# A planned long-convolution kernel with a second plan: order of the calls, large slots, PSUM rooms and the engine of its flexible copies

## The chip, the cores and the metric

The kernel runs on one core of one Trainium2 chip. The metric is the time in device microseconds (us) of one execution; the median of three runs is taken. A core has engines that work beside one another, each with its own queue of instructions: TensorE (PE, matrix products; "PEld" is the loading of its weights), VectorE (DVE), ScalarE (ACT), GpSimd (POOL) and SyncE (SP, which here only issues DMAs). SBUF is the on-chip memory of 128 partitions, PSUM the smaller memory into which PE writes and from which DVE or ACT must copy.

## The reference

The input u has 2048 positions and 448 channels. Two long convolutions of it are mixed by a gate:

```
g = sigmoid(sum(u * gate_w))                                  # per position
K = real(sum_n C_n * exp(dt * A_n * l) * dt * B_n)            # S4 kernel, 256 modes, l = 0..2047
a = causal_conv(u, K) + u * Dskip                             # "A"
kv = shift_conv(k, shift_k) * v                               # 4 taps
b = u * (causal_conv(kv, ssm_k) + kv * ssm_D)                 # "B"
out = g * a + (1 - g) * b
```

The causal convolutions are 2048 long; the reference does them by an FFT of twice that length.

## The kernel before, in words

**Work.** The 448 channels lie in four partition groups of 112; each convolution is done in four passes H = 0 to 3 of NC = 28 channels per group. `PLAN` (L37) gives the stages: T0 to T3 make the S4 kernel K of a pass, B0 to B3 are the passes of convolution B, A0 to A3 those of A, and four mixes m join the two.

- A **table** (`table`, L921; `KGen` L433, `Part` L520): 16 exponentials on ACT; four levels, each of phases on DVE, a Sin on ACT and a magnitude on DVE; products on DVE that fill the tables TQ and TP; then `sums` (L632), 448 small matmuls from TP and TQ, in seven groups of 64; then `gather`, matmuls that put the sums in order, and their copies. T3 is made in two halves. Exponentials and Sin need different tables on ACT, so each crossing has an ACT_TABLE_LOAD.
- A **convolution** (`conv_B` L911, `conv_A` L944): `spread` and `transform` (matmuls, each group ended by a copy from PSUM), `swapped` (copies of halves of the partitions over SP's DMA queue), `products` on DVE (two of 3584 elements), `stage_a` with copies, `stage_b` with an epilogue on DVE that uses the gate or u and writes back into natu or natv. A3, at the end, writes out in pieces (`store`, L890), half on SP's and half on ACT's queue.
- The **head**: modes and constants are loaded and prepared (`Consts` L176, `Modes` L650); DVE's first work needs c_pidx (L181), an iota of GpSimd. k is loaded by four transposing DMAs on SP (L774), three into natu and one into a large slot, with v and the kernel of B behind them on the same queue. The short convolution (L839) is eight groups of 56 matmuls, each ended by a DVE product with v into natv; natu is then free and u is loaded there.
- The **gate** (L858 to L871): one DVE product of 3584 elements (gwt), 112 matmuls, a copy (gx), one matmul, a Tanh on ACT and a scaling on DVE (gt). The first pass of A needs gt.

**What sets the order.** The program doesn't issue its calls as it makes them. `Order` (L125) notes all 6479 calls of all engines in a list, and `issue` (L132) issues them in the sequence of the string `ORDER`, whose numbers are places in that list; L137 is where each is issued, and so it is the line of nearly all instructions in the profile. Calls of one engine run in that sequence; between engines only semaphores for true dependences hold. `SLOTS` says for each of 54 large tiles which of seven SBUF slots q0 to q6 (3584 bf16 elements per partition) it takes (`Places.slot`, L153), and `ROOMS` says for each of 209 groups of matmuls which of four PSUM rooms of two banks it uses (`Places.room`, L157). `SIDES` says for each of 208 copies or scalings whether DVE ("V") or ACT ("S") does it (`Sides`, L336): copies of a room to SBUF, the phase's second half (`ahead`) and the sign of a level (`minus`).

The seven slots and four rooms tie the engines: a group of matmuls can start only when its room has been emptied, and a slot is written only when its last reader is done.

Of the kernel before, what the change touches and what calls it, by code (L numbers as in the profile page):

```python
# [35 lines left out]
NSLOT = 7  # L36
PLAN = (("T", 0), ("B", 0), ("B", 1), ("T", 1), ("B", 2), ("A", 0), ("T", 2), ("B", 3), ("A", 1), ("T", 3), ("A", 2), ("m", 0), ("m", 1), ("m", 2), ("m", 3), ("A", 3))  # L37
SLOTS = (
    "201031456232433120056615532041060303231061540604265013"
)  # L40
ROOMS = (
    "031230120122130132023010223312031201320001012121201100302332131110331210203301002313130323111031203103303210320132212000"
    "13111112310221033031032020012311212323010303033031323212102022201023121232131202010303130"
)
SIDES = (
    "SVSSSSSVSSSSSSSSSSSSSSSSSSSSSSSVSSSVSSVSSSSSSSSSSSSSSSSSSVVVVVSSSSSSSSSSSSSSSSSSSSSSSSSSSSSSSSSSSSSSSSSSSSSVVVVSSSSSSSSS"
    "SSSSSSSSSSSSSSSSSSSSSSVSSSSSSSSSSSSSSVSVVSVVSSSSSSVSSSSSSSSSSSVSSVVSSSSSSSSSVSVSVSSSVSSS"
)
ORDER = (
# [54 lines left out]
)  # L104

def after(tc, ins, before):
# [906 lines left out]
```

## Time and profile before

| what | value |
|---|---|
| median of the runs | 261.9 us (261.25, 261.9, 261.94) |
| span of the profiled execution | 257.9 us |
| instructions | 12431 |
| first DVE instruction, end of the last | 3.06 us, 247.6 us |
| end of the last matmul | 246.3 us |
| DMA | 26.44 MB, mean 103 GB/s |

The profile is of one execution; its span leaves out about 4 us that the runs' time includes. "Busy" is the time in which an engine has an instruction at work; since PE's matmuls are pipelined, its busy time isn't its peak. A row of a group gives the engine, the operation, out<-in by the program's names, the shapes, the count, then the busy time and the mean of one in ns, and the idle time of the engine ahead of it with what ended that. A row of a timeline begins with the start and the length in us. A row of the windows view gives the stretch, its length, and for each engine the busy time and the number of instructions, then the granted clock of PE (1.00 is full), the DMA share and GB/s.

### The profile page before, as it was taken

The page shows a single profiled execution, that of the slowest core. Times are in us where ns is not written, and L with a number is a line of the kernel's source. Part 1 is how long each engine was busy: PE and PEld are TensorE (multiplying, and loading weights), DVE is VectorE, ACT ScalarE, POOL GpSimd, SP SyncE. Part 2 cuts the span into 40 slices and gives each one's busy share as a digit, 9 for nine tenths or more (in the row PEclk, how much of TensorE's full clock was granted, in tenths as well). Part 3 has the DMA queues.
Part 4 walks back from the last instruction along what each step waited for, and adds up shares of the span by engine and source line. Part 5 has one row for each costly group of instructions (what it writes and reads, how often), then busy time and mean ns, then how long its engine had stood idle before and what let it go on. Part 6 is the DMA issues. An engine that isn't in the chain of part 4 may idle for free.

```text
span 257.9 us, 12431 instructions
## 1 busy us (share of the span) xinstructions
PE 208.9 (81%) x5631; PEld 188.6 (73%) x5631; DVE 237.4 (92%) x378; ACT 199.5 (77%) x278; POOL 30.5 (12%) x81
## 2 busy tenths in 40 slices
PE   0634784988779999998889998989999998999820
PEld 0511484978669898997879887888899897998810
DVE  4999999999999999999999999988999999998830
ACT  2299993089979999999999999989999975653300
POOL 8970001200000002100000021000031120000000
PEclk9995596899979999999999999997999999999975
DMA  6999983499861347475043055600462375120088
GB/s 167 212 164 216 165 178 74 82 171 159 139 157 32 47 106 144 79 167 91 7 99 104 3 102 95 149 24 3 111 110 38 57 145 131 29 51 4 3 163 125
DMA packets 58917, 26.44 MB, mean 103 GB/s; under 512 B 49520, under 2 KB 57200, under 8 KB 58864
## 3 DMA queue, kind: packets, MB, share of 16 engines
q1 hardware_dynamic: 52192, 18.65, 39.5%
q0 software_dynamic: 2160, 5.51, 12.2%
q10 hardware_dynamic: 4512, 1.49, 3.0%
q8 instruction: 44, 0.72, 1.2%
q14 instruction: 9, 0.07, 0.1%
HBM read 8.17 MB, written 2.52 MB: 41 GB/s over the span
## 4 chain that ended last, share of the span: by engine, by line
DVE 61%; PE 17%; issue 6%; DMA 5%; ACT 5%; SPq 1%; POOL 1%; DVEq 0%; ACTq 0%; POOLq 0%
DVE TP L137 18%; PE ps L137 17%; DVE q L137 15%; DVE TQ L137 15%; DVE natv L137 5%; ACT q L137 3%; DMA TP<-TP 3%; DVE ET L137 3%; DVE G L137 2%; DVE RK L137 1%; SPq L137 1%; DMA q<-q 1%; ACT ET L137 1%; DMA sk<-in_B_ssm_k_dram 1%; DVE hold L137 1%
## 5 line engine op out<-in xcount | busy, mean ns | idle before, releaser
L137 ACT CAST q<-ps 128x1024 bf16<-128x1024 f32 (+4 forms) x151 | 126.6, 929 | 23.9 <-PE ps L137 23.1
L137 PEld LDWEIGHTS <-q 128*128 128x128 bf16 (+2 forms) x720 | 52.3, 147 | 13.5 <-DMA q<-in_A_A_re_dram 8.4
L137 DVE TENSOR_TENSOR TQ<-TQ,ET 128x896 bf16<-128x896 bf16 (+2 forms) x70 | 45.5, 687 | 0.1
L137 PEld LDWEIGHTS <-natu 128*32 128x32 bf16 (+1 forms) x560 | 30.6, 183 | 8.9 <-issue 7.2
L137 PE MATMUL ps<-TP,TQ 128*32 128x32 bf16 x1792 | 33.3, 240 | 4.1 <-DVE TQ L137 2.6
L137 PE MATMUL ps<-q,s_W 128*128 128x112 bf16 (+1 forms) x544 | 33.8, 214 | 3.5 <-ACT q L137 3.4
L137 PE MATMUL ps<-sa_R,q 128*128 128x128 bf16 x448 | 33.3, 229 | 2.4 <-DVE q L137 1.0
L137 PEld LDWEIGHTS <-TQ 128*32 128x32 bf16 x1792 | 30.1, 153 | 6.7 <-DVE TQ L137 3.1
L137 DVE TENSOR_TENSOR q<-q,q 128x3584 bf16<-128x3584 bf16 (+1 forms) x22 | 32.4, 1513 | 1.2 <-ACT q L137 1.2
L137 PEld LDWEIGHTS <-s_W 128*128 128x128 bf16 x544 | 28.2, 100 | 6.5 <-issue 4.5
L137 DVE TENSOR_TENSOR TP<-TP,ET 128x1792 bf16<-128x1792 bf16 (+3 forms) x25 | 31.4, 1275 | 0.1
L137 POOL DMA_DIRECT2D TP<-TP x15 | 13.1, 914 | 153.8 <-PE ps L137 89.6
L137 PEld LDWEIGHTS <-G 128*128 128x128 bf16 x1024 | 27.9, 96 | 4.3 <-issue 2.5
L137 PE MATMUL ps<-q,G 128*128 128x28 bf16 x1024 | 28.5, 175 | 1.4 <-ACT q L137 1.4
L137 ACT ACTIVATE q<-hold 128x224 bf16<-128x224 f32 x64 | 22.4, 414 | 5.0 <-DVE hold L137 5.0
L137 PE MATMUL ps<-q,natu 128*32 128x336 bf16 (+3 forms) x336 | 17.8, 334 | 5.7 <-DVE natv L137 4.2
L137 ACT ACTIVATE ET<-q 128x1344 bf16<-128x1344 int16 (+1 forms) x12 | 17.2, 1457 | 1.4 <-DVE q L137 1.3
L137 PE MATMUL ps<-q,q 128*32 128x336 bf16 (+3 forms) x112 | 17.8, 334 | 0.0
L137 PE MATMUL ps<-Wc,natu 128*64 128x128 bf16 x224 | 15.5, 285 | 0.6 <-DVE q L137 0.6
L137 ACT CAST RK<-ps 128x448 bf16<-128x448 f32 (+1 forms) x16 | 11.5, 742 | 5.4 <-PE ps L137 5.4
L137 DVE TENSOR_TENSOR TQ<-TQ 128x448 bf16<-128x448 bf16 (+2 forms) x35 | 15.3, 446 | 0.1
L137 DVE CAST q<-ps 128x1024 bf16<-128x1024 f32 (+3 forms) x13 | 12.6, 978 | 2.4 <-PE ps L137 1.4
(81 smaller groups left out, 276.6 us busy)
## 6 DMA issues: line engine op xcount, KB each, us to landing
q<-q SPq DMA_DIRECT2D x64, 112.0 KB, 3.1
TP<-TP POOLq DMA_DIRECT2D x9, 448.0 KB, 5.0
natv<-in_B_v_dram SPq DMA_DIRECT2D x4, 448.0 KB, 7.3
sk<-in_B_ssm_k_dram SPq DMA_DIRECT2D x16, 112.0 KB, 3.8
natu<-in_A_u_dram SPq DMA_DIRECT2D x4, 448.0 KB, 10.2
TP<-TP POOLq DMA_DIRECT2D x6, 224.0 KB, 3.8
out_dram<-natv SPq DMA_DIRECT2D x8, 112.0 KB, 4.6
out_dram<-natv ACTq DMA_DIRECT2D x8, 112.0 KB, 4.5
```

The lines of the kernel that those rows point to most:

```text
L137: ins = f(*args, **kw)
```

## The change

Four strings are replaced, and nothing else: `SLOTS`, `ROOMS`, `SIDES` and `ORDER`. The calls and the PLAN stay; the same 6479 calls are issued in another order. In `SIDES` the number of V falls from 28 to 16: 21 copies or scalings go from DVE to ACT, 9 from ACT to DVE. Some of what moves in `ORDER`:

- c_pidx (call 1) stands ahead of the long iota (call 104) on GpSimd.
- T1's exponentials (2238 to 2253) stand among the head's calls on ACT, ahead of the first copies of the convolutions. One group of the short convolution (398 to 453) stands behind the first groups of B0's spread.
- T0's seven groups of sums (880 to 1327) stand in one block; T1's stand in two blocks.
- The gate's product and matmuls (688, 689 to 800) with what follows them (801 to 804) stand among A0's and T2's calls instead of T0's; 3614 is the first gated product of A0.

```diff
--- before.py
+++ after.py
@@ -36,71 +36,68 @@
 NSLOT = 7
 PLAN = (("T", 0), ("B", 0), ("B", 1), ("T", 1), ("B", 2), ("A", 0), ("T", 2), ("B", 3), ("A", 1), ("T", 3), ("A", 2), ("m", 0), ("m", 1), ("m", 2), ("m", 3), ("A", 3))
 SLOTS = (
-    "201031456232433120056615532041060303231061540604265013"
+    "021542305636511452202433460065313202216640354003105642"
 )
 ROOMS = (
-    "031230120122130132023010223312031201320001012121201100302332131110331210203301002313130323111031203103303210320132212000"
-    "13111112310221033031032020012311212323010303033031323212102022201023121232131202010303130"
+    "11223103012210302330220032331212210013320021033131021301111231323102110223230233221201311003220113302301102003222013"
+    "111030323310002132213200232132113303202300232012233311303200120101020221120311012032012033101"
 )
 SIDES = (
-    "SVSSSSSVSSSSSSSSSSSSSSSSSSSSSSSVSSSVSSVSSSSSSSSSSSSSSSSSSVVVVVSSSSSSSSSSSSSSSSSSSSSSSSSSSSSSSSSSSSSSSSSSSSSVVVVSSSSSSSSS"
-    "SSSSSSSSSSSSSSSSSSSSSSVSSSSSSSSSSSSSSVSVVSVVSSSSSSVSSSSSSSSSSSVSSVVSSSSSSSSSVSVSVSSSVSSS"
+    "SSSSSSSSSSSSSSSSSSSSSSSSSSSSSSSSSSSSSSSSSSSSSSSSSSSSSSSSSSSSSSSSSSSSSSSSSSSSSSSSSSSSSSSSSSSSSSSSSSSSSSSSSSSVSVVVSSSS"
+    "SSSSSSSSSSSSSSSSSSSVSSSSSSSSSSSSSSSSSSSSSSSVSVVVSSSSSSSVSSSSSSSSSSSSSSSVSSSSSSSSSSVSSSVVSVVS"
 )
 ORDER = (
-    "35 38 81 0 32-34 1 37 2 67-68 5 106 36 108 31 69 63 225 64 75 210 44 109 76 211 207 15 208 104 41 77 20 105 78 112 83 "
-    "107 74 6 71 202 70 66 212 72 209 73 221 214 50 82 30 65 111 219 110 79 17 140-155 215 84 216 116-117 203 222 91 204 "
-    "220 223 43 160-175 11 157 40 80 156 159 811 810 158 177-192 176 822 821 18 829 61 88 824 831 224 19 46 836 816 830 86 "
-    "809 113 823 805 837 12 194 817 89 808 812 22 120-121 807 14 813 226 806 39 45 85 818 123-124 193 825 4 3 25 130-131 "
...
-    "1536-1543 1844 861 2001-2008 874 62 1544 1967-1982 862 1843 2009 1841 1604-1611 2248 845 1983 1518-1525 865 878 1612 "
-    "1509-1516 866 2000 1622-1629 1526 873 1527-1534 876 1517 1631-1638 1630 688 1546 2010-2017 2238 1548 1613-1620 1639 "
-    "1551 1535 868 2019-2026 1552 867 2246 1842 689-800 2027 1547 2018 1550 870 2239 1545 871 3615 872 879 1549 2259 877 "
-    "2037-2044 875 1621 2270 1136-1199 2269 2271 2260 2045 2264 1264-1327 2262 1845 2272 115 2263 2273 1640-1647 801 2265 "
...
+    "1 104 69 207-208 2 70 214 32 75 63 106 209 216 67 7 108 39 68 64 31 140-147 215 26 210 105 24 211 0 212 19 65 28 "
+    "107 38 221 35 202 213 3 77 222 76 109 71-72 223-224 203 217-218 116 78 112 118 15 66 219 117 119 220 111 33-34 110 "
+    "113 204 22 79 156 805 817 808 37 811 6 807 157 813 819 73 148-155 158 74 159 36 160-175 816 829 20 806 50 837 21 10 "
+    "831 8 836 810 821 16 812 4-5 824 176 830 44 185-192 47 838 225 832 43 809 823 45 177-184 2254 194 29 822 839 193 12 "
...
+    "625 568 818 42 340 842 201 626-682 2249 40 227-282 57 1500-1507 2247 849 3615 2244 283 114 1508 1449-1464 1466-1481 "
+    "1465 1483-1498 1482 851 2262 398-453 511 683 1499 1527-1535 853 454 1844 857 1842 855 2263 1536-1543 1518-1525 "
+    "1587-1602 1526 856 1841 1544 873 1603 1570-1585 58 1586 1509-1517 858 874 1553-1569 2259 1604-1611 861 1612 1547 "
...
+    "2761 3627 3419 2762 688 3472-3479 3025-3040 3438-3453 3629 3421-3436 3645 3041 3454 3654 3652 3657 3659 3646 3480 "
+    "3455-3470 689-800 3661 3437 3658 3471 3663 801 3060-3067 4995 3078-3085 3068 4263 3660 802-803 2990 4264 4282-4297 "
+    "5002 3669 3665 2781-2820 4298 3672 3086 4299-4314 4996 3668 3548-3613 4315 3653 2821 2763-2779 804 2780 3662 3673 "
+    "3614 3051-3059 3664 4265-4280 2984 3069-3076 4281 3481-3546 4998 3077 4997 4999 4316-4324 5000 2839-2854 2822-2838 "
...
+    "5941-6007 6323-6356 6077 6357 6360 6358 6401-6434 6359 6440-6472 6362-6394 6435 6438 6361 6439 6437 6473-6476 6478 "
+    "6395-6396 6400 6436 6398 6397 6399 6477 "
 )
```

84 rows, old and new, of the table ORDER are left out of this document.

## The prediction

> **What bounds the kernel now.** I read the page's busy line and its chain of waits first, then stretches of the span.
>
> ```profile
> PE 208.9 (81%) x5631; PEld 188.6 (73%) x5631; DVE 237.4 (92%) x378; ACT 199.5 (77%) x278; POOL 30.5 (12%) x81
> ...
> DVE  4999999999999999999999999988999999998830
> ACT  2299993089979999999999999989999975653300
> ...
> DVE 61%; PE 17%; issue 6%; DMA 5%; ACT 5%; SPq 1%; POOL 1%; DVEq 0%; ACTq 0%; POOLq 0%
> ```
>
> VectorE (DVE) is the busiest engine and 61% of the chain. But the shares are means over unlike stages, so I cut the span where each table's small matmuls begin on TensorE (PE), by the rows of the tile TQ: T1 at 122.0, T2 at 166.4, the second half of T3 at 219.7 us.
>
> ```profile
> L137 PE MATMUL ps<-TP,TQ x127: 228/242/259, 122.0 to 124.0; 128*32 128x32 bf16 x127
> ...
> L137 PE MATMUL ps<-TP,TQ x44: 227/237/255, 166.4 to 167.0; 128*32 128x32 bf16 x44
> ...
> L137 PE MATMUL ps<-TP,TQ x96: 227/240/263, 219.7 to 221.9; 128*32 128x32 bf16 x96
> ```
>
> The windows view then gives, for each stretch, its length and the busy time of PE, PEld, DVE, ACT and POOL:
>
> ```profile
> 52.48:122.04 69.56, 62.54 (x1619) 57.90 (x1618) 68.41 (x92) 67.30 (x96) 2.59 (x3) 0.98 0.67 117
> 122.04:166.36 44.32, 40.04 (x1173) 36.85 (x1173) 44.14 (x60) 44.26 (x64) 2.56 (x3) 1.00 0.35 76
> 166.36:219.72 53.36, 50.88 (x1523) 47.57 (x1523) 50.95 (x101) 45.29 (x56) 5.82 (x8) 0.97 0.38 79
> 219.72:246.28 26.56, 25.25 (x776) 23.09 (x773) 23.73 (x29) 11.95 (x17) 0.00 (x0) 1.00 0.12 27
> 246.28:257.90 11.62, 0.00 (x1) 0.00 (x0) 1.33 (x4) 0.00 (x0) 0.00 (x0) 0.59 0.87 146
> ```
>
> No single engine bounds it. From T1 to T2, DVE and ScalarE (ACT) are both full (44.14 and 44.26 of 44.32) and PE loses 4.3 us. From T2 to T3, PE has 50.88 of 53.36: it loses 2.5 us, and ACT has room. In the last stretch PE sets the pace and loses 1.3 us. After PE come 11.6 us of last products and stores. So from T1 on the time is PE's work (40.04 + 50.88 + 25.25 = 116.2 us) plus 8.1 us that PE loses. Before T1, PE has 208.9 - 116.2 = 92.7 us of work in 122 us, and DVE, nearly never idle, decides.
>
> **The copies (SIDES).** 21 copies and scalings go from DVE to ACT, 9 go the other way. The groups by form give the prices.
>
> ```profile
> L137 ACT CAST q<-ps 128x1024 bf16<-128x1024 f32 x64 | 64.0, 1044 | 16.6 <-PE ps L137 16.2 <-DVE TP L137 0.3
> L137 ACT CAST q<-ps 128x896 bf16<-128x896 f32 x58 | 51.9, 951 | 4.3 <-PE ps L137 4.2
> L137 ACT CAST q<-ps 128x512 bf16<-128x512 f32 x20 | 12.4, 622 | 0.6 <-PE ps L137 0.4
> L137 ACT ACT_TABLE_LOAD x9 | 11.5, 1283 | 3.3 <-PEq L997 1.7 <-DVE q L137 1.4
> L137 DVE CAST q<-ps 128x1024 bf16<-128x1024 f32 x6 | 7.3, 1222 | 2.1 <-PE ps L137 1.1 <-ACT ET L137 1.0
> L137 DVE CAST q<-ps 128x896 bf16<-128x896 f32 x2 | 2.2, 1080 | 0.0
> L137 DVE TENSOR_SCALAR q<-q 128x672 int32<-128x672 int32 x6 | 3.5, 592 | 0.1
> L137 ACT CAST q<-ps 128x448 bf16<-128x448 f32 x5 | 2.6, 541 | 1.9 <-PE ps L137 1.9
> L137 ACT ACTIVATE ET<-ET 128x672 bf16<-128x672 bf16 x3 | 2.4, 788 | 0.0
> L137 DVE TENSOR_SCALAR ET<-ET 128x672 bf16<-128x672 bf16 x5 | 1.9, 379 | 0.0
> L137 ACT ACTIVATE q<-q,quarter 128x672 int32<-128x672 int32 x2 | 1.8, 875 | 0.0
> L137 DVE CAST q<-ps 128x448 bf16<-128x448 f32 x3 | 1.8, 616 | 0.0
> L137 DVE CAST q<-ps 128x512 bf16<-128x512 f32 x2 | 1.4, 691 | 0.3 <-PE ps L137 0.3
> ```
>
> DVE loses 6 x 1.222 (1024 wide) + 2 x 1.080 + 2 x 0.691 + 2 x 0.616 + 4 x 0.592 + 4 x 0.379 + the small gate copy 0.1 = 16.1 us. It gains one copy of 1024 and one of 896, one of 512, three of 448, one of 768 (between the rows of 512 and 896: 0.69 to 1.08, I take 0.95) and two scalings of 672: 1.22 + 1.08 + 0.69 + 1.85 + 0.95 + 0.76 = 6.6 us. Net -9.5; neighbours overlap by about a twentieth, so I take **-9.0 us for DVE**. ACT gains 6 x 1.044 + 2 x 0.951 + 2 x 0.622 + 2 x 0.541 + 4 x 0.875 + 4 x 0.788 + 0.2 = 17.3, loses 6.6 at its own prices (1.04 + 0.8 + 0.62 + 0.95 + 3 x 0.54 + 2 x 0.79) and, as its new order crosses between two tables once more, gains a tenth table load, 1.3: 12, or with overlap about **+11 us for ACT**. PE's work stays 208.9. DVE's saving lies on a path in the first half; ACT's addition is covered only where ACT has idle time, that is at the head and after 200 us, and not from 122 to 166.
>
> **The head.** The order puts the small iota that DVE waits for ahead of the long one on GpSimd, and T1's 16 exponentials into a stretch where ACT waited.
>
> ```profile
> 0.84 1.99 POOL L137 IOTA TP<- 32x2048 bf16 x1 [0.40 <-POOLq L997]
> 2.90 0.13 POOL L137 IOTA c_pidx<- 128x1 int32 x1
> ...
> 3.06 0.15 DVE L137 TENSOR_SCALAR TP<-c_pidx 128x1 int32<-128x1 int32 x1 [3.06 <-POOL c_pidx L137]
> ...
> 40.89 2.08 DVE L137 TENSOR_TENSOR natv<-ps,natv 128x896 bf16<-128x896 f32 x2
> ...
> 42.03 0.61 PE L137 MATMUL ps<-q,natu 128*32 128x448 bf16 x3 [4.17 <-DVE natv L137]
> ...
> 52.48 2.88 ACT L137 CAST q<-ps 128x1024 bf16<-128x1024 f32 x3 [11.67 <-PE ps L137]
> ```
>
> DVE can start about 2 us earlier. Ahead of its first eviction of the k-shift convolution the new order has 35.3 us of DVE work where the old had 37.3 (summed over the trace's durations). So PE's 4.17 us of idling shrinks, and the eviction itself comes about 3 to 4 us earlier. ACT then starts the convolutions' copies at 45 to 48 instead of 52.5. Against it: the fourth transposed load of k now uses a slot that frees later, and it holds SP's queue (v and the ssm kernel behind it) some 3 to 5 us; with DVE's first eviction at 37 to 39 this stays covered, and it costs up to 3 us if not. Between the ends -7 and -1 at the head I take -4.5.
>
> The clock is the other part of this: the windows after the idle time show half of it.
>
> ```profile
> 42.00:44.00 2.00, 1.97 (x36) 1.67 (x39) 2.00 (x3) 0.00 (x0) 0.00 (x0) 0.50 0.86 163
> ...
> 48.00:50.00 2.00, 2.00 (x80) 2.00 (x75) 2.00 (x2) 0.00 (x0) 0.00 (x0) 1.00 0.93 172
> ```
>
> PE did 36 of these matmuls in 2 us at a granted clock of 0.50, and 80 at 1.00, so the slow stretch cost some 2 us. [...]
>
> **The stages, by PE's work left.** I ran the three sums of busy time through the new order. DVE's work ahead of the end of T1's table falls from 117.2 to 110.8 us: three copies (3.0), the gate's large product, which goes later (2.0), and smaller moves. With DVE 2 us earlier that is 8.4 us; the ring of rooms emptied by ACT, now busy from 46 on, leaves about 4.5. So T1's small matmuls begin at 117.5. But this is partly borrowed: PE has 121.0 us left there instead of 116.2, since the gate's matmuls and a part of the convolutions now stand behind T1.
>
> ```profile
> 65.99 2.01 DVE L137 TENSOR_TENSOR q<-gw,one 128x3584 bf16<-128x3584 bf16 x1
> ...
> L137 PE MATMUL ps<-natu,q 128*32 128x64 bf16 x112 | 3.6, 301 | 0.3 <-ACT q L137 0.3
> ```
>
> If PE lost the same 8.1 us, its end would be 117.5 + 121.0 + 8.1 = 246.6 us, where it is 246.3 now: **no gain at all**. The forecast so hangs on what PE loses.
> - T1 to T2: 48.9 us of PE work, 48.3 of DVE, 48.8 of ACT. Three engines with the same load, and the gate's round (DVE, PE, ACT, PE, ACT, DVE) among them: PE must lose something. Nothing lost is one end, 7 the other (below); I take 3.5, a little under the 4.3 now, since now DVE and ACT have 10% more work than PE there. T2 at 117.5 + 52.4 = 169.9.
> - T2 to T3: PE 48.0, DVE 45.1 (now 50.88 and 50.95). DVE no longer stands level with PE: a loss of 0.5 instead of 2.5. T3 at 218.4.
> - The rest: 24.1 and the same 1.3: PE ends at 243.8.
> - Stores and last products as now, 11.6: span 255.4, or 2.5 us less than 257.9. What ACT gets more behind T2 is covered by its idle time, for it is busy 14.71 and 9.47 us of 20 there:
>
> ```profile
> 200.00:220.00 20.00, 18.86 (x601) 17.30 (x599) 19.63 (x38) 14.71 (x19) 2.58 (x3) 1.00 0.52 108
> 220.00:240.00 20.00, 19.52 (x619) 17.99 (x612) 18.05 (x22) 9.47 (x15) 0.00 (x0) 1.00 0.12 28
> ```
>
> Slots and rooms add no work; their new numbers act by waits alone, and those are in the losses above. The swaps on SP's queue stand behind waits for PE and DVE that the sums put ahead of their readers; if one is late it costs its landing time, 3.1 us by the page's DMA rows:
>
> ```profile
> q<-q SPq DMA_DIRECT2D x64, 112.0 KB, 3.1
> ```
>
> **The rivals.**
> 1. DVE's gain arrives in full: nothing but PE's own work counts from T1 to T3. PE ends at 117.5 + 121.0 + 1.3 = 239.8, span 251.4, run 255.4. For it: DVE has 9 us less to do and is 61% of the chain. Against: DVE alone would allow 257.9 - 9 = 248.9, but PE's 121 us behind T1 do not; and ACT has no idle time from T1 to T2.
> 2. The early gain is given back: PE loses as much as now, 246.6, span 258.2, run 262.2. No change. For it: the sum of DVE's and ACT's work grows by 2 us, and PE's is the same.
> 3. **Slower: ACT is the new pacemaker between T1 and T2.** It has 48.8 us of work there and is also held by the gate: by the sums of busy time ACT reaches the copy of the gate's sums 2.4 us before PE ends its 112 matmuls, and DVE reaches the first gated product of conv A about 4 us before the gate's value is there, and what ACT copies next waits for DVE. If these 6.4 us come on top of ACT's 48.8, T2 begins at 172.7; with losses as now behind it (2.5 and 1.3) PE ends at 172.7 + 50.5 + 25.4 = 248.6, span 260.2, run 264.2. It decides from a T2 later than 170.4 (losses as now behind) to 172.4 (losses of my forecast). For it: ACT stood at 44.26 of 44.32 already; against: the gate's round can be covered by the copies behind it.
>
> **How the numbers follow.** The profiled execution had 257.9 us of span, and the median of the runs is 261.9, so 4.0 us lie around the span; I add the same: 255.4 + 4.0 = 259.4. Two kernels of this length can be told apart from about 0.3%, 0.8 us: faster is under 261.1, slower over 262.7. Chances: my forecast 0.43 (from 257.4 to 261.1), rival 1 0.17, rival 2 0.13, rival 3 0.27. That makes 0.60 faster, 0.13 the same, 0.27 slower. The range goes from rival 1 (255.4, its own spread a little lower) to rival 3: 255.0 to 264.4; left out are about 0.05 below and 0.12 above, where a late swap or the late load of v adds to rival 3. By itself the forecast's range is 257.4 to 261.1.
>
> **What would show it.** In the profile of the changed kernel: DVE about 228 and ACT about 210 busy; DVE's first instruction near 1; the first copy of the convolutions on ACT before 48 and no clock of 0.5 after 38; T1's small matmuls near 117.5, T2's near 170, T3's second half near 218.4, PE's last at 243.8. Wrong would be: a T2 after 172 with ACT's idle time in the 120s put down to PE or DVE (rival 3); a T1 not before 120 (the head's gain lost, as by a late load of v or by ACT); PE idle by over 2 us between T2 and T3 with DVE named.

## The result: the changed kernel is slower, by 22 us

| | before | after |
|---|---|---|
| median of the runs | 261.6 us | 283.8 us (282.8 to 285.7) |
| ratio, 95% interval | | 1.086 (1.080 to 1.092) |
| span of the profiled execution | 257.9 us | 282.6 us |
| first copy of the convolutions on ACT | 52.5 us | 44.3 us |
| small matmuls of T0, T1, T2, second half of T3 begin | 74.0, 122.0, 166.4, 219.7 | 72.0, 127.1, 181.2, 240.6 |
| PE ends | 246.3 us | 272.3 us |

Some executions run slower as a whole, whatever the kernel; the medians and ratios below leave those out.

The forecast was 259.4 us in a range from 255.0 to 264.4. The page of the kernel after, busy times, slices and chain:

```profile
PE 218.3 (77%) x5631; PEld 195.9 (69%) x5631; DVE 229.8 (81%) x366; ACT 212.3 (75%) x291; POOL 30.4 (11%) x81
...
DVE  8999999999929739999867998985839797747950
ACT  5669998999908998999769999935889976356100
...
PEclk9999999959955997999899999997599999869955
...
PE 42%; ACT 29%; DVE 12%; issue 9%; SPq 2%; DMA 2%; ACTq 0%; DVEq 0%; POOL 0%; POOLq 0%
```

DVE has 7.6 us less to do and ACT 12.8 us more, where the sums gave 9 and 11. But DVE's and ACT's rows of digits now have holes, the deepest of them at the same place (2 and 0 tenths in the twelfth slice, 78 to 85 us), and the chain has gone from DVE (61%) to PE (42%) and ACT (29%). The windows view, cut where the tables' small matmuls begin:

```profile
72.00:127.10 55.10, 42.65 (x1177) 39.81 (x1177) 42.97 (x60) 44.55 (x62) 2.56 (x3) 0.85 0.49 93
127.10:181.20 54.10, 48.76 (x1360) 45.23 (x1360) 48.24 (x64) 49.43 (x69) 2.56 (x3) 0.97 0.28 58
181.20:240.60 59.40, 51.09 (x1490) 46.66 (x1489) 45.41 (x90) 44.24 (x56) 5.79 (x8) 0.91 0.35 72
240.60:272.30 31.70, 26.26 (x751) 24.09 (x749) 22.44 (x29) 11.74 (x15) 0.00 (x0) 0.85 0.12 26
```

From T0 to T1 all three engines have 10 us and more of idle time in 55.1 us. Before, that stretch was 48.0 us long and none of the three had more than 2.3 us idle in it:

```profile
74.00:122.04 48.04, 45.81 (x1291) 42.74 (x1291) 46.89 (x64) 45.91 (x69) 2.59 (x3) 0.96 0.50 101
```

So the place to look at is where each of these stretches begins: at the 448 small matmuls of a table. The same windows for the sums of T0, T1 and T2 alone, before:

```profile
74.00:87.70 13.70, 13.17 (x540) 12.01 (x541) 12.58 (x23) 12.19 (x23) 0.00 (x0) 0.88 0.38 79
122.00:132.60 10.60, 9.58 (x473) 8.77 (x474) 10.42 (x21) 10.55 (x11) 0.00 (x0) 1.00 0.13 28
166.40:181.20 14.80, 13.71 (x529) 12.97 (x529) 12.93 (x25) 12.94 (x17) 0.00 (x0) 0.88 0.12 28
```

and after:

```profile
72.00:85.30 13.30, 7.80 (x450) 7.32 (x451) 7.44 (x13) 5.19 (x7) 0.00 (x0) 0.74 0.53 74
127.10:137.10 10.00, 8.42 (x458) 7.88 (x457) 9.37 (x10) 8.42 (x9) 0.00 (x0) 0.83 0.03 7
181.20:194.10 12.90, 9.06 (x466) 8.46 (x466) 8.08 (x13) 5.05 (x5) 0.00 (x0) 1.00 0.10 24
```

The sums take about as long in both kernels. Before, PE did 540 matmuls in T0's 13.7 us, 92 of them other groups, and ACT and DVE worked 12 us beside it. After, PE does the block of 448 and nothing else, 7.8 us of work in 13.3, and ACT works 5.2 and DVE 7.4. The timelines of PE, ACT and DVE at T0's block:

```profile
72.01 2.24 PE L134 MATMUL ps<-TP,TQ 128*32 128x32 bf16 x131 [0.26 <-ACT q L134]
76.91 2.19 PE L134 MATMUL ps<-TP,TQ 128*32 128x32 bf16 x128 [2.66 <-issue]
80.64 2.17 PE L134 MATMUL ps<-TP,TQ 128*32 128x32 bf16 x128 [1.54 <-issue]
84.09 1.12 PE L134 MATMUL ps<-TP,TQ 128*32 128x32 bf16 x61 [1.29 <-issue]
...
85.27 0.54 ACT L134 CAST RK<-ps 128x448 bf16<-128x448 f32 x1 [8.07 <-PE ps L134]
...
85.34 0.63 DVE L134 TENSOR_TENSOR TQ<-hold,ET 128x896 bf16<-128x896 bf16 x1 [5.90 <-PE ps L134]
```

PE does 131 of the small matmuls in 2.24 us, then stands idle for 2.66 with nothing to wait for that the profile shows ("issue"), does 128, stands again, and so on. ACT has emptied its last room at 76.3, has ended all other work by 77.2 and then waits 8.07 us for the sums; DVE has one product left, which ends at 79.4, then waits 5.90 us, for it may not write the next table into TQ before the sums have read it.

(The long iota behind which c_pidx stood is call 81; the section on the change gave 104, which is a DVE call that reads c_pidx. And where that text speaks of seven groups of 64 small matmuls, several groups stand side by side in the kernel before: its runs on PE are 128, 64, 64, 128, 64 long in T0, 192, 64, 64, 128 in T1 and 128, 64, 64, 64, 128 in T2. After, they are 448 in T0, twice 224 in T1 and in T2, and 224 in each half of T3.)

### The profile page after: what moved, and what is told of

It is laid out like the page before. It is cut to its first block, busy times and chain, and to the rows that moved or that the text cites. A ratio compares the mean times of both kernels' runs of the same rounds, so it can differ in the third digit from the quotient of the medians.

```text
span 282.6 us, 12420 instructions
## 1 busy us (share of the span) xinstructions
PE 218.3 (77%) x5631; PEld 195.9 (69%) x5631; DVE 229.8 (81%) x366; ACT 212.3 (75%) x291; POOL 30.4 (11%) x81
## 4 chain that ended last, share of the span: by engine, by line
PE 42%; ACT 29%; DVE 12%; issue 9%; SPq 2%; DMA 2%; ACTq 0%; DVEq 0%; POOL 0%; POOLq 0%
PE ps L134 42%; ACT q L134 21%; DVE TP L134 4%; DVE q L134 3%; ACT ET L134 3%; SPq L134 2%; DVE TQ L134 2%; DMA q<-q 2%; ACT L134 1%; DVE natv L134 1%; ACT s_W L134 1%; ACT TQ L134 1%; DVE natu L134 1%; ACT RK L134 1%; DVE RK L134 1%
## 5 line engine op out<-in xcount | busy, mean ns | idle before, releaser
L134 ACT CAST q<-ps 128x1024 bf16<-128x1024 f32 (+3 forms) x156 | 131.9, 923 | 15.7 <-PE ps L134 14.9
L134 PEld LDWEIGHTS <-q 128*128 128x128 bf16 (+2 forms) x720 | 55.7, 150 | 18.0 <-DMA q<-in_A_A_re_dram 5.9
L134 PE MATMUL ps<-q,s_W 128*128 128x112 bf16 (+1 forms) x544 | 36.4, 220 | 10.0 <-ACT q L134 8.2
L134 PE MATMUL ps<-TP,TQ 128*32 128x32 bf16 x1792 | 31.6, 241 | 13.9 <-issue 13.1
L134 PE MATMUL ps<-sa_R,q 128*128 128x128 bf16 x448 | 37.4, 248 | 5.5 <-DVE q L134 3.1
L134 PEld LDWEIGHTS <-s_W 128*128 128x128 bf16 x544 | 30.4, 104 | 13.6 <-issue 11.4
L134 POOL DMA_DIRECT2D TP<-TP x15 | 13.1, 915 | 168.5 <-PE ps L134 104.1
L134 PE MATMUL ps<-q,natu 128*32 128x336 bf16 (+3 forms) x336 | 16.2, 311 | 0.7 <-ACT TQ L134 0.7
L134 PE MATMUL ps<-q,q 128*32 128x336 bf16 (+3 forms) x112 | 16.1, 310 | 0.0
L134 PE MATMUL ps<-Wc,natv 128*64 128x128 bf16 x224 | 15.4, 287 | 0.9 <-issue 0.6
L134 PEld LDWEIGHTS <-natv 128*64 128x64 bf16 x224 | 14.5, 213 | 1.6 <-issue 0.8
```

The source lines that it names most:

```text
L134: ins = f(*args, **kw)
```

## The experiments

**Theory 1**: the blocks cost the time. In a block PE feeds neither ACT nor DVE, and its own supply of instructions runs out. **Theory 2**: ACT, with some 11 us more copies, is the new pacemaker (my rival 3). Each run is given with its ratio to the kernel before on the same chip; an absolute difference is against 260.4 to 262.7 us. The runs with quarter and wide in their names leave matmuls out, so their output is not that of the reference.

| run | edit | median | ratio (95%) |
|---|---|---|---|
| b_block | before, sums in blocks | 284.9 | 1.092 (1.085 to 1.100) |
| b_pairs | before, groups joined two and two | 262.6 | 1.009 (1.005 to 1.012) |
| b_224 | before, runs of 224 | 276.5 | 1.056 (1.049 to 1.063) |
| b_block0 | before, T0's block alone | 268.3 | 1.031 (1.017 to 1.044) |
| a_quarter | after, a quarter of the sums' matmuls | 261.1 | 0.993 (0.988 to 0.997) |
| b_quarter | before, a quarter of them | 259.7 | 0.987 (0.983 to 0.992) |
| a_wide | after, half of them, thrice as wide | 277.4 | 1.055 (1.051 to 1.060) |
| b_blockwide | b_block, half of them, thrice as wide | 280.4 | 1.074 (1.067 to 1.081) |
| a_split | after, blocks cut to 64 | 288.6 | 1.105 (1.098 to 1.111) |
| a_fill | after, blocks cut to 128 | 282.4 | 1.082 (1.075 to 1.088) |
| b_sidesa | before, SIDES of after | 268.1 | 1.026 (1.020 to 1.032) |
| a_sidesb | after, SIDES of before | 294.6 | 1.121 (1.113 to 1.128) |
| b_pidx | before, c_pidx first | 261.7 | 1.004 (1.001 to 1.008) |
| b_pool | before, 16 small constants first | 259.1 | 0.991 (0.987 to 0.995) |

### Blocks in the kernel before: b_block, b_pairs, b_224, b_block0

Only `ORDER` changes, and in it only the place of the tables' small matmuls. T0's part in b_block:

```diff
...
-    "2037-2044 875 1621 2270 1136-1199 2269 2271 2260 2045 2264 1264-1327 2262 1845 2272 115 2263 2273 1640-1647 801 2265 "
+    "1621 2270 1136-1199 1264-1327 1008-1071 880-943 1072-1135 944-1007 1200-1263 2269 2271 2260 2045 2264 2262 1845 2272 "
...
```

> The kernel before, with the seven chunks of 64 small matmuls of each table put in one block at the place of the first; nothing else moves. Theory 1 (a long run of these small matmuls empties PE's supply of instructions, and meanwhile PE gives ACT and DVE nothing): the block of T0 takes about 13 us instead of 8 with idle time put down to issue, ACT and DVE wait behind it, and the run takes 270 to 282 us. Theory 2 (ACT, which got 11 us of copies, is the new pacemaker): the blocks hardly matter, 261 to 265 us.

284.9 us: the blocks alone make the kernel before as slow as the kernel after. ACT's waits for PE double; by the waits of the kernel before they were 23.1 us (`ACT q L137 <- PE ps L137`), in b_block:

```profile
ACT q L135 <- PE ps L135: 47.1, 15, 11.6
...
DVE q L135 <- PE ps L135: 16.0, 4, 7.9
```

and the windows of b_block, first T0's block, then the stretches between the tables as above:

```profile
74.00:83.70 9.70, 7.46 (x449) 7.08 (x450) 3.25 (x12) 3.56 (x4) 0.00 (x0) 0.82 0.20 62
...
74.00:129.50 55.50, 48.62 (x1295) 44.93 (x1295) 46.98 (x64) 46.06 (x69) 2.59 (x3) 0.88 0.43 87
129.50:180.10 50.60, 42.15 (x1173) 38.90 (x1173) 44.37 (x60) 44.95 (x66) 2.56 (x3) 0.93 0.33 71
180.10:240.10 60.00, 53.06 (x1522) 49.22 (x1522) 50.88 (x101) 44.75 (x54) 5.76 (x8) 0.86 0.31 64
```

ACT and DVE stand idle for 6.1 and 6.4 us inside T0's block, and the stretch to T1 grows by 7.5 (55.5 against 48.0); the next two grow by 6.3 and 6.6. The time is above the expected 270 to 282 us, though T0's block took 9.8 us, not the 13 that were expected.

> The kernel before, with the chunks of the small matmuls joined two and two (runs of 128 instead of 64). Theory 1, if the supply holds some 128 of them as the trace of after suggests (a first idle gap behind 131): 261 to 264 us, without idle gaps inside a pair. If every joining costs in proportion, 265 to 270. Theory 2: 262.

262.6 us, 2 us more. But the edit changes less than the expectation says: runs of 128 and one of 192 were there before. Joined two and two the runs are 128, 128, 128, 64 in T0 and T2, 256, 128, 64 in T1. Idle time inside them there was (2.3 us in all put down to issue, 1.55 of it in the run of 256). So this run shows that such runs cost little, not from which length on they cost.

> The kernel before with its chunks of small matmuls joined to runs of 224 (four chunks, then three; T3's halves in one run each). Between the measured +2 us of runs of 128 and +24 us of whole blocks of 448. If the cost comes with what ACT and DVE can do from the four rooms that are full when a run begins (about 4 us of copies), a run of 224 (4 us or more) is where it begins: 266 to 272 us. If it grows with the length alone: 270 to 275.

276.5 us, 14 more: above both ranges, 1.5 us over the upper end of the one for a cost that grows with the length. The stretches from T0 to T1, T1 to T2 and T2 to the second half of T3 grew by 4.7, 3.9 and 4.0 us, where b_pairs has 2.0, 1.8 and -0.8 and b_block 7.5, 6.3 and 6.6. That looks more like a cost that grows with the length than like a threshold at the four rooms; the run of 256 in b_pairs, in whose stretch only 1.8 us were lost, fits neither well. The first run of 224 in T0 had no idle time in it (3.71 us), so the supply of instructions isn't what made that one costly:

```profile
73.99 3.71 PE L136 MATMUL ps<-TP,TQ 128*32 128x32 bf16 x224 [1.65 <-DVE TQ L136]
```

> The kernel before with T0's sums alone in one block. If each block costs by itself, about 7.5 us as the stretch from T0 to T1 grew with all of them: 267 to 271 us, and the later stages as before. If a later stage wins it back, under 265; if the blocks only cost together, 262.

268.3 us: some 7 us (1.7 to 4.4%) for one block of five, as expected. T1's small matmuls begin at 130.6 instead of 122.0 in the profiled execution, and the 8.4 us that PE's end is late there (254.7 against 246.3) are there already at T1. Nothing is won back later.

### The sums nearly left out: a_quarter, b_quarter

Three of four small matmuls are skipped; `SUMS` lists their places among the calls.

```diff
...
-            for f, args, kw in self.calls[int(a):int(b or a) + 1]:
+            for i in range(int(a), int(b or a) + 1):
+                f, args, kw = self.calls[i]
+                if any(lo <= i <= hi and not ((i - lo) % 16 < 4) for lo, hi in SUMS):
+                    done += 1
+                    continue
...
```

> The kernel after with three of four of the small matmuls of each table's sums left out (112 instead of 448 a table, the sums are then not those of the reference); order, slots, rooms and sides as in after. Theory 1 (the blocks cost the time, by supply and by starving ACT and DVE): 252 to 259 us, level with or under the kernel before with the same left out. Theory 2 (ACT's copies, the late gate, the slots): 270 us or more, as far above its counterpart as after is above before.

> The kernel before with the same three of four small matmuls left out. It is the counterpart: PE loses 1344 matmuls of about 17 ns, some 23 us of work, but DVE has the same, so 252 to 258 us by all theories.

261.1 and 259.7 us, both 2 us above their ranges. The kernel after gains some 23 us (1.086 to 0.993), the kernel before 3 (0.987), by the same 1344 matmuls left out. So before, the sums lay beside other work and cost nearly nothing, and after, they stand alone. It also tells what the rest of the change is worth, the new slots, rooms and copies of ACT included: nothing, or a loss of one us. So theory 2 can't explain the 22 us: ACT has the same copies in a_quarter (211.3 us busy). The stretch from T1 to T2 in a_quarter, and the same in b_quarter:

```profile
120.50:171.70 51.20, 44.48 (x1028) 40.96 (x1028) 47.75 (x62) 49.14 (x69) 2.85 (x4) 0.93 0.31 63
```

```profile
122.60:166.90 44.30, 37.04 (x837) 33.90 (x837) 44.13 (x60) 44.14 (x63) 2.85 (x4) 0.88 0.38 82
```

ACT has 49.14 of 51.20 us: here it is the pacemaker, and the 2 us that a_quarter is ahead at T1 are given back.

### Supply or length: a_wide, b_blockwide, a_fill, a_split

In the wide versions the skipping keeps every second set of four, and the rest writes 96 columns:

```diff
...
-                        rhs = bass.AP(r0.tensor, r0.offset, [list(r0.ap[0]), [32 * m0 + (1 - 2 * c) * m0, 2], [2 * m0, 16]])
+                        rhs = bass.AP(r0.tensor, r0.offset, [list(r0.ap[0]), [0, 3], [32 * m0 + (1 - 2 * c) * m0, 2], [2 * m0, 16]])
...
```

> The kernel after with half of the small matmuls left out and the other half three times as wide (96 columns), so that PE is busy with a block about as long but with half the instructions (the sums are not those of the reference). If the supply of instructions is what a block costs (1a): the idle time put down to issue in the blocks goes, and the run takes 262 to 272 us. If a block costs because PE gives no other work meanwhile, however it is supplied (1b): 278 to 286 us with the same waits of ACT. The length of the blocks in the trace says how even the exchange is.

277.4 us, 6 to 8 less than after (6.4 by the times, 8 by the ratios), just under the range of 1b. The idle time is gone from the block, as PE's timeline shows,

```profile
72.73 9.77 PE L141 MATMUL ps<-TP,TQ 128*32 128x96 bf16 x224 [0.48 <-ACT q L141]
```

which makes the sums of the five tables and halves together 41.1 us long instead of 47.0: 5.9 us shorter, for 6 to 8 us of the run. The exchange is not even, so this alone doesn't part supply from length.

> The kernel before with each table's sums in one block, half of these matmuls left out and the other half three times as wide (96 columns; the sums are not those of the reference). In the trace of after's wide version such a block of 224 took 9.8 us without idle time, as long as a block of 448 in the kernel before with blocks (9.8 us, 2.3 of it idle at the joints). If only the length counts: 281 to 288 us, like the blocks of 448. If the supply of instructions counts beyond the length: 265 to 276 us.

280.4 us, 4.5 less than b_block, with the same lengths (T0's block 9.8 and 9.7 us, all five 39.7 and 39.5). So with the length held, half of the instructions save 4 to 5 of the 24 us, and some 19 remain with the length alone. The expectation for "only the length" began at 281; it is close to that, not on it. The run also bounds another candidate, a low clock of PE behind the blocks: b_blockwide has the mean granted clock of the kernel before (0.929 in both profiled executions) and is 19 us slower all the same. What it saves against b_block may be the clock, which is 0.880 there.

For a_fill and a_split, the blocks in `ORDER` of the kernel after are cut. T0's part in a_fill:

```diff
...
-    "2270 2036 2018 1906-1913 2271 1613-1621 1552 1924-1932 2884 2269 2272-2273 2267-2268 880-1103 115 1104-1327 2260 "
+    "2272-2273 2267-2268 880-1007 115 2260 1650 2274 1933-1940 1008-1135 1914 2261 1328 1923 2275 3635 3634 3632-3633 3636 "
...
```

> The kernel after, with its blocks of small matmuls cut to chunks of 64 and other groups of matmuls that don't depend on them put between; the calls that depend on a chunk follow it, all else as in after. Theory 1: most of the loss goes, 264 to 272 us, and the idle time put down to issue falls from 13 us to under 5. Theory 2: 278 to 284 us, since ACT's work is the same.

288.6 us: a miss, no gain but a loss of 5, though the idle time of the sums put down to issue did fall, from 13.1 to 3.1 us. The window of T0's sums in a_split says why:

```profile
72.20:92.70 20.50, 15.55 (x520) 13.92 (x521) 7.68 (x14) 11.89 (x15) 0.00 (x0) 0.75 0.34 47
```

ACT now has work, but the sums end only at 92.7, for PE does other groups in the joints and waits there, 2.71 us of it for a product of DVE. DVE, which from 79.9 on has nothing else in its queue than the next table, works 7.68 us of 20.5:

```profile
92.80 0.63 DVE L134 TENSOR_TENSOR TQ<-hold,ET 128x896 bf16<-128x896 bf16 x1 [12.92 <-PE ps L134]
```

In the kernel before DVE had two products of 3584 elements, three copies and pieces of the next table to do between 77 and 87; in after's order its two products are done by 79.4. Cutting the blocks thus isn't enough: DVE's order must have work to put beside the sums.

> The kernel after with its blocks cut to runs of 128 small matmuls and one other group of matmuls, the next that doesn't depend on them, put into each joint. If the idle time at the joints (2.7, 1.5 and 1.3 us in T0) is the supply of instructions, these groups run in it nearly for nothing: 272 to 280 us, some 4 to 12 under after, and under the same cut into runs of 64. If each joint only delays the end of the sums, for which DVE waits: 284 to 290 us, like the cut into runs of 64.

282.4 us, 1.5 less than after, not clear of its interval and between the two ranges. The idle time put down to issue inside the sums fell from 13.1 to 4.5 us, and the sums of T0 took 15.6 us instead of 13.2: what was filled was paid back by the later end.

### The copies' engines: b_sidesa, a_sidesb

```diff
...
-    "SVSSSSSVSSSSSSSSSSSSSSSSSSSSSSSVSSSVSSVSSSSSSSSSSSSSSSSSSVVVVVSSSSSSSSSSSSSSSSSSSSSSSSSSSSSSSSSSSSSSSSSSSSSVVVVSSSSSSSSS"
+    "SSSSSSSSSSSSSSSSSSSSSSSSSSSSSSSSSSSSSSSSSSSSSSSSSSSSSSSSSSSSSSSSSSSSSSSSSSSSSSSSSSSSSSSSSSSSSSSSSSSSSSSSSSSVSVVVSSSS"
...
```

> The kernel before with the SIDES of after at the same calls (copies that go to ACT or DVE by the list of after), order, slots and rooms as before. Theory 1: 260 to 266 us, ACT's added 11 us are partly covered. Theory 2: 270 us or more, with ACT named for PE's waits.

> The kernel after with the SIDES of before at the same calls; order, slots and rooms as in after. Theory 1: 280 to 288 us, the blocks are still there. Theory 2 (ACT is the new pacemaker): 268 to 276 us, since ACT has its 11 us less to do.

268.1 us, 7.5 more, between the two theories' ranges; and 294.6 us, 9 to 11 more than after, above both. Giving ACT its old share back makes the kernel after worse. With a_quarter this rules theory 2 out as the cause of the 22 us. Each list does best with its own order; that a copy put on the other engine stands in a queue whose neighbours were not chosen for it is my reading and wasn't tested.

### The head: b_pidx, b_pool

The first line of `ORDER` in b_pool; b_pidx only puts call 1 ahead of 81.

```diff
-    "35 38 81 0 32-34 1 37 2 67-68 5 106 36 108 31 69 63 225 64 75 210 44 109 76 211 207 15 208 104 41 77 20 105 78 112 83 "
+    "35 38 1-2 5 31 63 225 75 109 15 41 20 6 71 212 221 214 81 0 32-34 37 67-68 106 36 108 69 64 210 44 76 211 207-208 104 "
...
```

> The kernel before with one call moved: the iota of c_pidx on GpSimd goes ahead of the long iota. DVE starts about 2 us earlier. If DVE's first half sets the time, as the prediction has it, 259.5 to 261 us against some 261.5; if the 2 us are lost in the head (the loads of the modes arrive at the same time), no change.

261.7 us: no gain (0.4% slower, if anything), though DVE began at 0.99. Its waits show where the 2 us went, to the next constant behind the same iota:

```profile
DVE TP L135 <- POOL quarter L135: 2.2, 1, 2.2
```

> The kernel before with 16 small constants of GpSimd (iotas and memsets that DVE waits for) ahead of the first long iota, not only c_pidx. If DVE's start and what it waits for next were the only hold: DVE's work comes 2 us earlier, T0's small matmuls at 72, and the run takes 259.5 to 260.5 us against some 261.5. If the head is held by the loads of the modes or by ACT, no change.

259.1 us (0.991): **faster than the kernel before** by about 1 to 2 us, a small gain, and so faster than both. T0's small matmuls begin at 72.6 instead of 74.0, T1's at 120.5 instead of 122.0, and PE ends at 245.0 instead of 246.3. What DVE wins ahead of T0 arrives at the end. It is part of what the kernel after has, without the rest.

## Why the prediction was wrong

**What held.** DVE's and ACT's busy times (228 and 210 forecast, 229.8 and 212.3 measured). The head: DVE's first instruction at 0.99, its first eviction at 37.2 (37 to 39 forecast), the convolutions' copies from 44.34 instead of 52.48, T0's small matmuls at 72.0, and, at that place, the clock. The kernel after has 1.00 from 40 to 50, with 0.39 us of idle time on PE,

```profile
40.00:50.00 10.00, 9.61 (x278) 8.95 (x273) 9.23 (x13) 9.20 (x15) 0.00 (x0) 1.00 0.19 49
```

where the kernel before had 0.55 and 0.50 from 40 to 46. The sign "no clock of 0.5 after 38" failed later: the clock was 0.50 from 58 to 64, from 80 to 92 and in later places. That a shorter idle gap keeps the full clock, as that sign has it, was an assumption of mine, and no run shows how short is enough: the head of the kernel before had 0.50 behind a gap of 4.17 us, the head of the kernel after 1.00 with 0.04 us of idle time from 30 to 44, and T0's block of the kernel after 0.50 with no gap over 2.66. The gate's round cost what rival 3 gave it, 6.3 us of 6.4: ACT waited 2.2 us for its sums, DVE 2.6 for its value and 1.5 more, for a copy of ACT, ahead of the first gated product.

**The step that failed** is "The stages, by PE's work left". It carried three sums of busy time and took a loss of PE only behind T1: "T1's small matmuls begin at 117.5", then 3.5, 0.5 and 1.3. T1 began at 127.1, and 9.6 us were lost before the first loss that I had counted, though T0's sums began 2 us earlier than before. The stretches behind it took 54.1, 59.4 and 31.7 us for the 52.4, 48.5 and 25.4 of the forecast. The front of the document said that T0's sums now stand in one block, and no step of the prediction put a price on that: the block was worth its matmuls, as if it didn't matter what lies between them. The runs show the price in the kernel before: some 7 us for T0's block alone (b_block0), 24 for all (b_block), where the whole change costs 22. In a block the three sums don't run beside one another. ACT has four rooms to empty and then nothing, DVE has what its queue holds ahead of the next table, and PE itself does 448 matmuls in 13.2 us instead of 8. A sum of busy times can't see this; the rows that could have shown it are those of the kernel before, where T0's 448 came in five runs of 64 or 128 with 92 other matmuls among them.

**The rivals.** Rival 3 had the right sign with a wrong cause: ACT is full from T1 to T2 (49.1 of 51.2 in a_quarter), which undoes the early gain, but it didn't bring the 22 us, since a_quarter has the same copies without them, and giving the copies back made the kernel slower. Rival 2 (the early gain given back) is what the rest of the change does: 261.1 against 259.7 without most of the sums. Rival 1 and the forecast's gain from T2 to T3 had their piece of truth, for that stretch is 50.4 us in a_quarter where b_quarter has 53.6, and it was spent from T1 to T2.

**DVE's 2 us at the start**, which I put into T1's place, need all the small constants, as b_pool shows; c_pidx alone gave nothing.

**The 4.0 us around the span** was too much: it set one execution's span beside the median of others. In each of the later executions the time is 1.7 to 2.0 us above its own span. With 2.0 the same sum gives 257.4 us, which changes nothing in the miss.

**What stays open**: that the blocks cost the kernel after its 22 us rests on the same blocks' cost in the kernel before and on a_quarter; no order of after's own sums was found that is faster. How the cost parts there between PE's supply of instructions, the length and the clock isn't known. With the length held, fewer instructions and a higher clock together were worth 4 to 5 of 24 us in b_block, but the gaps also make the blocks longer (47.0 us after, 39.7 in b_block), and no run had a block of 448 without idle time. What a run of 224 costs by each wasn't parted either. And the seven slots and four rooms were not tried apart from the order.

## What to carry to other kernels

Sums of busy time bound a plan only as long as each engine finds work at each moment: look in a new order for long runs of one engine's instructions from which no other engine gets anything, and price such a run by what the others have queued at its start (here four rooms, some 4 us of copies: an estimate from the 1.03 us of one of 128x1024 on ACT). Work that is free when it is scattered can be the most expensive part when it is put together: the same matmuls cost 3 us in one order and 23 in the other. And before an early start is counted as a gain, follow the queue that gave it to the next thing that is waited for in it.

## What the runs showed of the hardware

In a long run of these small matmuls, each with its weight load, PE stood idle at times with nothing to wait for but the issue: in T0's block of the kernel after for 2.66, 1.54 and 1.29 us, between runs of 131, 128, 128 and 61, the full ones 2.2 us long. How many went before the first gap differed: 224, 144 and 208 in the first runs of T1, T2 and T3 after. Behind a gap there were never more than 128 in this kernel. The page's row "q8 instruction" (packets, MB, share) goes with that; here it is for after, for a_quarter with 1344 of 5631 matmuls less, and for a_wide with 896 less:

```profile
q8 instruction: 44, 0.72, 1.1%
...
q8 instruction: 33, 0.54, 0.9%
...
q8 instruction: 37, 0.61, 1.0%
```

As these matmuls and their loads go, so do the packets: 2688 instructions for 11 of them, 1792 for 7. An estimate from this is some 250 instructions a packet, or about 128 small matmuls with their loads. In T0's block of the kernel after these packets started at 73.8, 78.0 and 81.7, 4.2 and 3.7 us apart, where PE takes 2.2 us for 128; PE went on at 76.91, 80.64 and 84.09. That PE's gaps are waits for these packets fits all this; the profile names no releaser for them, so it isn't shown. Half as many instructions, three times as wide, ran 9.77 us without a gap (a_wide).

The granted clock fell in the block though no gap there was as long as the 4.17 us in the head of the kernel before. The windows of the kernel after:

```profile
74.00:76.00 2.00, 0.25 (x16) 0.13 (x9) 2.00 (x3) 2.00 (x3) 0.00 (x0) 1.00 0.86 111
...
78.00:80.00 2.00, 1.10 (x71) 0.94 (x63) 1.44 (x1) 0.00 (x0) 0.00 (x0) 0.59 0.10 19
80.00:82.00 2.00, 1.36 (x92) 1.36 (x94) 0.00 (x0) 0.00 (x0) 0.00 (x0) 0.50 0.03 8
82.00:84.00 2.00, 0.81 (x52) 0.66 (x44) 0.00 (x0) 0.00 (x0) 0.00 (x0) 0.50 0.00 0
```

It stayed at 0.50 up to 92. From 76 to 84 PE was busy 40 to 70% of each window, and its longest idle gap in the block was 2.66 us. In T2's block of the same kernel (181.2 to 194.1), with gaps of 1.01, 1.01 and 1.78 us put down to issue, the clock was 1.00. From which gap or share of idle time on the clock falls, these runs don't show. At 0.50 the small matmuls took no longer, 2.17 us for 128 where 131 had taken 2.24 at 1.00; others did: from 86 to 92 the mean of one of ps<-RK,ga_sel 128x224 was 386 ns and of ps<-sa_R,q 308, against 261 and 229 over the whole kernel before. PE's busy time is 218.3 us against 208.9 for the same matmuls.
